# Strided attention pairs: two residues in one product of 36 columns

## The chip, the cores and the metric

The kernel runs on one core of a Trainium2 chip. The metric is the device time of one execution in microseconds (us). The engines are TensorE (PE, with PEld for its weight loads), VectorE (DVE), ScalarE (ACT), GpSimd (POOL) and SyncE (SP), which issues most of the DMAs.

## The reference

Attention with 8 batches, 8 heads, 576 positions and 64 features a head, followed by a gated feed-forward layer. Half of the heads see the last 32 positions, the other half those positions that have the same residue modulo 32.

```python
def _attn_ref(q, k, v):
    B, H, S, D = q.shape                       # 8, 8, 576, 64
    scores = (1.0 / np.sqrt(D)) * np.matmul(q, k.transpose(0, 1, 3, 2))
    pos = np.arange(S)
    rel = pos[:, None] - pos[None, :]
    mask_local = (rel >= 0) & (rel < 32)
    mask_strided = (rel >= 0) & (pos[None, :] % 32 == pos[:, None] % 32)
    masks = np.stack([mask_local if h < H // 2 else mask_strided for h in range(H)], axis=0)
    scores = np.where(masks[None], scores, -1000000000.0)
    scores = scores - np.max(scores, axis=-1, keepdims=True)
    attn = np.exp(scores)
    attn = attn / (np.sum(attn, axis=-1, keepdims=True) + 1e-09)
    return np.matmul(attn, v).astype(np.float32)

def _moe_ref(x, w_in, w_out):                  # x: 4608 x 512, w_in: 512 x 2048, w_out: 2048 x 512
    h = x @ w_in
    g = h * np.clip(h + 3.0, 0.0, 6.0) / 6.0
    return (g @ w_out).astype(np.float32)
```

## The kernel before, in words

**Attention** goes by pairs of heads: four pairs a batch, two local and two strided, 32 in all. `kept_pair(g)` records all the steps of one pair. A strided pair's sequence is sorted by residue: 32 residues with 18 positions each (`NPOS`), padded to 32 rows on the query side. Eight blocks of four residues make 128 rows. For one block, one residue and one head there is one score product, 32 queries by 18 keys (L676, in `scores`): 8 * 4 * 2 = 64 products. Head `j` takes rows 64j to 64j+63 of the array and writes bank `ps[j]`. Batches 0 and 1 are done in ways of their own (`early`, `apart`), which the change leaves. From batch 3 on (`ADDED`) the causal mask `mtri` is added on DVE while the scores leave their bank (`keep`, L687); in batch 2 a product with `eye` puts it into the bank first (L665), and a copy takes the scores out (L689 on ACT, L691 on DVE).

Then follow, on a tile `e` with 2 * 8 * 18 = 288 elements a partition: maximum (`most`, L730, DVE), subtraction (`less`, L752, POOL), exponential (L755, ACT), sum (`total`, L758, DVE), reciprocal (L762 and L763, DVE), scaling (`norm`, L767, POOL). Four 32-row transposes a head (L813, DVE) turn the result into the tile `at` for one head and `at2` for the other, four residues on the diagonal of a 128 by 128 block. The values are one product for each block and head, with 128 rows, 64 weight columns and 72 columns moved (L869, `both_mm`): 16 products into two banks, the first four blocks in one and the last four in the other. ACT and DVE write them out into `x`, or `xf` from batch 3 on (`keep_x`, L458, L469, L472). A local pair has twelve transposes (L808) and window products (L441) in their place. In batch 1 (`apart`), the strided values are 64 columns of weights over 18 rows with 18 columns moved (L881, `half_mm`), in two halves with a small DVE copy between them, the fence (L885).

**Feed-forward.** Batches 0 to 2 run alone (`ffn`): wide products of 128 by 512 in groups of three, L1030 to L1032 into the two banks `ph`, and L963 to L965 into the four banks `acc`. A gate on ACT and DVE (L1065, L1069) empties a `ph` bank into `u`; `split_g` makes a high part on ACT (L996) and a low part on POOL (L999). From 353 us on, batches go in pairs (`ffn_pair`, three pairs `0`, `1`, `2`), with seven combined products where there were eight (L1204 to L1206, two banks as well), whose sums DVE forms in `htmp` (L1223). `split_g` is told by the names `0a`, `0b`, `1a`, `1b` which half it serves; the last pair has a splitting routine of its own and doesn't call it.

**Order.** Every step is recorded by `op(engine, cost, function, reads, writes, due, ...)`; `Plan.emit` then simulates the engines with these costs and due times and fixes one order for each engine, ahead of time. Some steps may go to either of two engines, as the plan finds them free. On the chip each engine runs its order strictly, and waits for semaphores. Due times follow from `T0` (the start of the first feed-forward), `TILE` and the lists above. So a changed cost shifts many steps by some places on every engine.

Of the kernel before, what the change touches and what calls it, by code (L numbers as in the profile page):

```python
# [20 lines left out]
P = 128  # L21
# [4 lines left out]
NQB = 6  # L26
NPOS = 18
RB = 7
SB = RB * NPOS
# [15 lines left out]

T0 = 36.0
TILE = 98.5
# [31 lines left out]
PORT = ("DVE", "POOL")  # L79
IDLE_DVE = ("2a", "2b")  # L80

# [131 lines left out]
def attention_ffn(ctx: ExitStack, tc, q, k, v, w_in, w_out, out):  # L213
# [40 lines left out]
    mturn = const.tile([PAD, 2 * PAD], BF16, name="mturn")  # L254
    mtri = const.tile([P, NPOS], BF16, name="mtri")
    mwhole = const.tile([QB, NQB, 2 * PAD], BF16, name="mwhole")
    left = [const.tile([P, B * LEFT], F32, name=f"left{c}") for c in range(NCC)]
# [10 lines left out]
    def masks():  # L268
# [16 lines left out]
        for a in range(4):  # L285
# [3 lines left out]
                base=0, pattern=[[-1, NPOS]], channel_multiplier=1)  # L289

    op("POOL", 0.8, identity, writes=[("ident",)], due=-100)
    op("POOL", 2.2, masks, reads=[("ident",)], writes=["const"], due=-22)

# [185 lines left out]
    def kept_pair(g):  # L479
# [146 lines left out]
        n = QB if loc else P  # L626
        w = 2 * PAD if loc else NPOS
        cols = nblk * w

        def e_both():  # L630
            t = e_tile()
            return t[:QB, :, :cols].rearrange("p j (u x) -> p j u x", x=w) if loc else \
                t[:, :, base:base + 8 * PAD].rearrange("p j (u x) -> p j u x", x=PAD)[:, :, :, :w]
# [25 lines left out]
        def scores():  # L659
            if spare_e and loc:  # L660
                tiles["e", loc] = new(wp, ekey, [P, 2, cols], F32, f"e{nm}")
            ps = [psum(sb[j], f"ps{nm}{j}")[:n, :cols].rearrange("p (u x) -> p u x", x=w) for j in range(2)]
            m = (mband if loc else mtri).unsqueeze(1).to_broadcast([n, nblk, w])
            for j in range(0 if added else 2):
                nc.tensor.matmul(ps[j], eye[:n, :n], m, start=True, stop=False)  # L665
            if loc and not added:
                for j in range(2):
                    m = mturn if shifted else mfirst
                    nc.tensor.matmul(ps[j][:PAD, 0, :m.shape[1]], eye[:PAD, :PAD], m, start=False, stop=False)
            for i in range(nblk):  # L670
                for a in range(n // PAD):
                    for j in range(2):
                        own = slice(D * j, D * j + D)
                        r = i * (n // PAD) + a
                        k0 = max(r, 1 if shifted else 0) * (PAD if loc else NPOS)
                        nc.tensor.matmul(ps[j][PAD * a:PAD * a + PAD, i], qk_of("q")[own, PAD * r:PAD * r + PAD],  # L676
                                         qk_of("k")[own, k0:k0 + w], start=added, stop=added or i == nblk - 1)
# [4 lines left out]
        def keep(e, j):  # L682
            ps = ps_of(j)
            if j == 0:
                new(ap, stkey, [P, 2, 2, 8], F32, f"st{nm}")
            if added:
                nc.vector.tensor_tensor(out=e_own(j), in0=ps, in1=mwhole if loc else mtri.unsqueeze(1).to_broadcast([n, nblk, w]), op=ALU.add)  # L687
            elif e == "ACT":
                nc.scalar.copy(e_own(j), in_halves(ps))  # L689
            else:  # L690
                nc.vector.tensor_copy(e_own(j), in_halves(ps))  # L691
# [28 lines left out]
        if early and not loc:  # L720
            sb = []
        else:
          op("PE", ((1.35 if loc else 1.35) if early else (1.1 if loc else 1.35) if added else 1.5) * slow, scores, reads=["const", qkey, kkey, *both_halves], writes=[*sb, ekey, ekey1, stkey],
             take=sb, due=sd - 1000, room=0.0 if early else ROOM, mode="s", words=4 * 2 * (18 if loc else 32) + 6)
        for j in range(len(sb)):
# [72 lines left out]
        def transposes(j):  # L798
            def tr():
                e = e_whole(j)  # L800
                if apart:
                    nc.vector.transpose(tiles["atk"][:, odd, j], e)
                    return
                at = tiles[akeys[j]]
                if loc:
                    for a in range(3):
                        for h in range(2):
                            nc.vector.transpose(at[PAD * (a + h):PAD * (a + h) + PAD, :, PAD * a:PAD * a + PAD],  # L808
                                                e[PAD * a:PAD * a + PAD, :, PAD * h:PAD * h + PAD])
                else:  # L810
                    for a in range(4):
                        rows = slice(PAD * a, PAD * a + PAD)
                        nc.vector.transpose(at[rows, :, rows], e[rows])  # L813

            op("DVE", 6 * 0.37 if loc else 0.45 if apart else 4 * 0.435, tr, reads=[ekey, ekey1, *home], writes=[akeys[j]], due=due - 2 + j)
# [48 lines left out]
        else:  # L864
            def both_mm():
                ps, vt = [psum(vb[h], f"pv{nm}{h}") for h in range(2)], tiles[vkey]
                for i in range(8):
                    for j in range(2):
                        nc.tensor.matmul(ps[i // 4][D * j:D * j + D, i % 4 * P:i % 4 * P + 4 * NPOS], vt[:, j, i],  # L869
                                         (tiles[akeys[i % 2]][:, 4 * j + i // 2] if early else tiles[akeys[j]][:, i]).rearrange("p (a m) -> p a m", a=4)[:, :, :NPOS], start=True, stop=True)  # L870

            def half_mm(u):
                if u == 0:
# [14 lines left out]
            if apart:  # L888
                op("PE", 0.65 * slow, partial(half_mm, 0), reads=[*akeys, *home, vkey], writes=vb, take=vb,
                   due=due - 1002, room=0.0 if early else ROOM, mode="v", words=130)  # L890
                op("DVE", 0.16, fence, reads=vb, writes=[stkey], due=due - 1002)
                op("PE", 0.65 * slow, partial(half_mm, 1), reads=[*akeys, *home, vkey], writes=[*vb, *xk, lk], due=due - 1001, mode="v", words=130)
            else:
                op("PE", 1.3 * slow, both_mm, reads=[*akeys, vkey], writes=[*vb, *xk, lk], take=vb,
                   due=due - 1001, room=0.0 if early else ROOM, mode="v", words=64)
            puts = []
            for h in range(2):
                def what(ps, m):
                    if apart:
                        return ps[:, :16 * NPOS].rearrange("c (t a m) -> c t a m", t=RUN, a=2)[..., m]  # L900
                    return ps.rearrange("c (t x) -> c t x", x=P)[:, :, :4 * NPOS].rearrange("c t (a m) -> c t a m", a=4)[..., m]

                def place(x, h=h):
                    if apart:
                        return x.rearrange("c (m a z t) -> c t a z m", t=RUN, a=2, z=2)[:, :, :, h]
                    return x.rearrange("c (m a t) -> c t a m", t=RUN, a=4)[:, 4 * h:4 * h + 4]
# [640 lines left out]
    op("POOL", 0.1, first_tiles, writes=["plain"], due=-30)  # L1547
    zero(("e",), ap, [P, 2, 5 * P], F32, 1.45, -12, "e")
    op("POOL", 0.0, lambda: None, reads=[("e",)], writes=["el", "es", "el1", "es1"], due=-12)
# [36 lines left out]
    def homes():  # L1586
        tiles["sq"] = new(wp, homes_at[0], [P, 8 * P], F32, "sq")
        tiles["sv"] = new(wp, homes_at[1], [P, 2, 8, D], F32, "sv")
        tiles["at2"] = new(wp, homes_at[2], [P, 8, P], F32, "at2")
        tiles["at"] = new(ap, ("at",), [P, 8, P], F32, "at")  # L1590
    hk = ["sq", "sv", "at2", "at"]
# [61 lines left out]
```

## Time and profile before

| | |
|---|---|
| time, median of 3 runs | 885.27 us (883.56 to 891.9) |
| the profiled execution's own time | 883.06 us |
| its span, first to last instruction | 881.3 us |
| granted TensorE clock | 1.000 |
| PE / DVE / POOL / ACT busy | 98% / 71% / 52% / 46% of the span |
| matrix products | 8046 records |
| DMA | 190.73 MB, mean 216 GB/s |

The profile shows one execution. An engine's busy time is the sum of its instructions without overlap; a matrix product's row has an end that is modelled, so two products that follow each other overlap in it, and the pace is read from their starts. A row of the timeline gives start, duration, engine, line, operation, output and inputs, the part of the array (`64*32`: 64 rows, 32 weight columns), the moved tile and how many of them were merged. A row of the groups gives the same with busy time, mean ns of one, and idle time of the engine before them with its releasers. One fp32 product shows as two records there.

### The profile page before, as it was taken

To read this page: it belongs to the slowest core of one execution; us is meant where nothing else is said; L and a number is where in the kernel's file an instruction comes from. 1 tells how busy PE (TensorE), PEld (TensorE's weight loads), DVE (VectorE), ACT (ScalarE), POOL (GpSimd) and SP (SyncE) were. 2 spreads that over 40 slices of the span, in tenths; PEclk is the share of its full clock that TensorE was granted. 3 is DMA by queue.
4 is the path that set the end of the run, shared out by engine and by line. 5 is a ranking of instruction groups with operands and counts; after the bars stand their busy time and mean duration, and the time that the engine had idled before them with its cause. 6 is when DMAs were issued, how large, how long until landed. Compare 5 with 4: busy or idle time off the path is not lost.

```text
span 881.3 us, 20423 instructions
## 1 busy us (share of the span) xinstructions
PE 867.9 (98%) x8046; PEld 712.3 (81%) x8046; DVE 626.6 (71%) x1014; ACT 401.9 (46%) x723; POOL 458.4 (52%) x402
## 2 busy tenths in 40 slices
PE   9999999999999999999999999999999999999998
PEld 6777788788787888788888888888887888888898
DVE  6999977678888878766768733546658756566872
ACT  4787564333344434534345632544455343333730
POOL 5797666329777638222234844434559973131300
PEclk9999999999999999999999999999999999999999
DMA  7988836875789899887774688789738789565632
GB/s 186 318 234 210 194 99 182 253 199 166 209 236 237 239 231 224 255 232 205 215 218 142 200 283 219 252 236 254 246 130 316 264 286 328 168 214 192 188 126 70
DMA packets 231825, 190.73 MB, mean 216 GB/s; under 512 B 164401, under 2 KB 195121, under 8 KB 231729
## 3 DMA queue, kind: packets, MB, share of 16 engines
q1 hardware_dynamic: 231572, 189.12, 74.1%
q8 instruction: 64, 1.05, 0.5%
q10 hardware_dynamic: 156, 0.29, 0.1%
q14 instruction: 33, 0.26, 0.1%
HBM read 148.47 MB, written 40.89 MB: 215 GB/s over the span
## 4 chain that ended last, share of the span: by engine, by line
PE 87%; DVE 5%; DMA 3%; SPq 2%; POOL 2%; issue 1%; ACT 1%; DVEq 0%; ACTq 0%; POOLq 0%
PE ph L1204 9%; PE ph L1205 8%; PE ph L1206 8%; PE ph L1030 5%; PE acc L963 4%; PE ph L1032 4%; PE ph L1031 4%; PE acc L965 4%; PE acc L964 4%; PE az L1425 3%; PE az L1423 3%; PE az L1424 3%; PE ps L676 3%; DMA rawi<-in_moe_w_in_dram 2%; PE pv L441 2%; PE acc0a L963 2%
## 5 line engine op out<-in xcount | busy, mean ns | idle before, releaser
L1204 PE MATMUL ph<-xc,wi 128*128 128x512 f32 x336 | 134.4, 400 | 2.4 <-DVE u L1069 1.8
L1205 PE MATMUL ph<-xc,wi 128*128 128x512 f32 x336 | 131.4, 391 | 0.3 <-issue 0.3
L1206 PE MATMUL ph<-xc,wi 128*128 128x512 f32 x336 | 131.0, 390 | 0.0
L1223 DVE TENSOR_TENSOR htmp<-ph,htmp 128x512 f32<-128x512 f32 x72 | 49.5, 688 | 75.1 <-PE ph L1206 70.2
L999 POOL TENSOR_TENSOR g<-u,g 128x512 fp32r<-128x512 f32 x48 | 64.7, 1349 | 55.8 <-ACT g L996 27.4
L1030 PE MATMUL ph<-x,wi 128*128 128x512 f32 x192 | 78.5, 409 | 0.9 <-DVE u L1069 0.9
L1204 PEld LDWEIGHTS ph<-xc,wi 128*128 128x128 f32 x336 | 63.1, 188 | 19.2 <-DVE htmp L1217 2.8
L963 PE MATMUL acc<-wo,g 128*128 128x512 f32 x192 | 76.5, 398 | 0.5 <-ACT g L996 0.5
L965 PE MATMUL acc<-wo,g 128*128 128x512 f32 x192 | 75.0, 391 | 0.9 <-POOL g L999 0.9
L1031 PE MATMUL ph<-x,wi 128*128 128x512 f32 x192 | 75.0, 391 | 0.0
L1032 PE MATMUL ph<-x,wi 128*128 128x512 f32 x192 | 75.0, 390 | 0.0
L964 PE MATMUL acc<-wo,g 128*128 128x512 f32 x192 | 74.9, 390 | 0.0
L1206 PEld LDWEIGHTS ph<-xc,wi 128*128 128x128 f32 x336 | 63.1, 188 | 14.1 <-issue 0.5
L1205 PEld LDWEIGHTS ph<-xc,wi 128*128 128x128 f32 x336 | 63.3, 188 | 11.0
L808 DVE STREAM_TRANSPOSE atloc<-e 32x192 f32<-32x192 f32 x168 | 61.8, 368 | 7.9 <-POOL e L767 5.5
L1065 ACT ACTIVATE u<-ph,three 128x512 f32<-128x512 f32 x48 | 33.0, 687 | 73.7 <-PE ph L1032 73.5
L752 POOL TENSOR_TENSOR e<-e,st 128x288 f32<-128x288 f32 (+1 forms) x30 | 34.2, 1139 | 61.2 <-DVE st L730 61.1
L1215 ACT COPY htmp<-ph 128x512 f32<-128x512 f32 x56 | 32.8, 587 | 50.1 <-PE ph L1206 49.0
L813 DVE STREAM_TRANSPOSE at<-e 32x256 f32<-32x256 f32 x112 | 48.6, 434 | 5.2 <-POOL e L767 3.9
L996 ACT CAST g<-u 128x512 fp32r<-128x512 f32 x48 | 29.6, 620 | 38.0 <-DVE u L1069 28.9
L1030 PEld LDWEIGHTS ph<-x,wi 128*128 128x128 f32 x192 | 36.0, 187 | 10.7 <-DVE u L1069 2.3
L767 POOL TENSOR_TENSOR e<-e,st 128x288 f32<-128x288 f32 (+1 forms) x30 | 33.9, 1130 | 18.7 <-DVE st L763 15.3
(318 smaller groups left out, 2311.7 us busy)
## 6 DMA issues: line engine op xcount, KB each, us to landing
wi<-wid SPq DMA_DIRECT2D x84, 512.0 KB
wo<-wod SPq DMA_DIRECT2D x83, 512.0 KB
rawi<-in_moe_w_in_dram SPq DMA_DIRECT2D x16, 512.0 KB
rawo<-in_moe_w_out_dram SPq DMA_DIRECT2D x16, 512.0 KB
wod<-wo SPq DMA_DIRECT2D x16, 512.0 KB
wid<-st SPq DMA_DIRECT2D x64, 128.0 KB
qn<-in_q_dram SPq DMA_DIRECT2D x112, 72.0 KB
kn<-in_k_dram SPq DMA_DIRECT2D x112, 72.0 KB
```

The costliest lines, as they stand in the source:

```text
L808: nc.vector.transpose(at[PAD * (a + h):PAD * (a + h) + PAD, :, PAD * a:PAD * a + PAD], e[PAD * a:PAD * a + PAD, :, PAD * h:PAD * h + PAD])
L963: nc.tensor.matmul(acc, gh, woh, start=fc == 0, stop=False)
L964: nc.tensor.matmul(acc, gh, wol, start=False, stop=False)
L965: nc.tensor.matmul(acc, gl, woh, start=False, stop=end)
L999: on(e).tensor_tensor(out=to(1), in0=tiles[uk], in1=tiles[gk[0]].bitcast(F32), op=ALU.subtract)
L1030: nc.tensor.matmul(ph, wih, xh, start=n_ == 0, stop=False)
L1031: nc.tensor.matmul(ph, wih, xl, start=False, stop=False)
L1032: nc.tensor.matmul(ph, wil, xh, start=False, stop=n_ == NCC - 1)
L1204: nc.tensor.matmul(ph, w[:, j, 0], x[:, 0], start=u in (0, 1, 3) and j == 0, stop=False, skip_group_check=u in (2, 4, 5, 6))
L1205: nc.tensor.matmul(ph, w[:, j, 0], x[:, 1], start=False, stop=False, skip_group_check=u in (2, 4, 5, 6))
L1206: nc.tensor.matmul(ph, w[:, j, 1], x[:, 0], start=False, stop=j == 1, skip_group_check=u in (2, 4, 5, 6))
L1223: nc.vector.tensor_tensor(out=tiles[s.key], in0=tiles[bank], in1=tiles[s.key], op=ALU.add)
```

## The change

For the strided pairs of batches 2 to 7 (`wide`, 12 pairs) one score product takes two residues: 64 queries by 36 keys (`TWO`), 32 products in place of 64. Half of each result is masked, by the mask `mtwo`, built on POOL at the start. `e` then has 2 * 8 * 36 = 576 elements a partition. The transposes take each residue's own 18 columns (and 14 beside them) out of it. `at` and `at2` shrink to blocks of two residues, 64 rows high, and the values become 32 products with 64 rows, 64 weight columns and 36 columns moved (`two_mm`), with all first halves of the blocks in one bank and all second halves in the other.

The recorded costs of the two product steps go down, from 1.35 to 0.8 (batch 2: 1.5 to 1.05) and from 1.3 to 0.75, `T0` goes from 36 to 37, and `IDLE_DVE`, the names for which `split_g` may use DVE for the low part, from `2a`, `2b` (which never reach `split_g`) to `0b`, `1a`, `1b`. Every other cost that depends on the number of columns follows by its formula.

```diff
+TWO = 2 * NPOS
-T0 = 36.0
+T0 = 37.0
-IDLE_DVE = ("2a", "2b")
+IDLE_DVE = ("0b", "1a", "1b")
...
+        nc.gpsimd.memset(mtwo, NEG)
+        for a in range(4):
+            m = slice(PAD * a, PAD * a + PAD)
+            nc.gpsimd.tensor_copy(mtwo[m, a % 2 * NPOS:a % 2 * NPOS + NPOS], mtri[m])
...
-        w = 2 * PAD if loc else NPOS
+        wide = not loc and b > 1
+        w = 2 * PAD if loc else TWO if wide else NPOS
...
-            m = (mband if loc else mtri).unsqueeze(1).to_broadcast([n, nblk, w])
+            m = (mband if loc else mtwo if wide else mtri).unsqueeze(1).to_broadcast([n, nblk, w])
...
-            for i in range(nblk):
+            for i in range(nblk if wide else 0):
+                for a in range(2):
+                    for j in range(2):
+                        own, r = slice(D * j, D * j + D), 4 * i + 2 * a
+                        nc.tensor.matmul(ps[j][2 * PAD * a:2 * PAD * a + 2 * PAD, i], qk_of("q")[own, PAD * r:PAD * r + 2 * PAD],
+                                         qk_of("k")[own, NPOS * r:NPOS * r + TWO], start=added, stop=added or i == nblk - 1)
+            for i in range(0 if wide else nblk):
...
-          op("PE", ((1.35 if loc else 1.35) if early else (1.1 if loc else 1.35) if added else 1.5) * slow, scores, ...
+          op("PE", (0.8 if added else 1.05) if wide else (1.35 if early else 1.1 if added else 1.5) * slow, scores, ...
...
+                elif wide:
+                    for a in range(4):
+                        rows, at0 = slice(PAD * a, PAD * a + PAD), base + a % 2 * NPOS
+                        nc.vector.transpose(at[rows, :, PAD * (a % 2):PAD * (a % 2) + PAD],
+                                            e_tile()[rows, j, at0:at0 + nblk * TWO].rearrange("p (u x) -> p u x", x=TWO)[:, :, :PAD])
...
+            def two_mm():
+                vt = tiles[vkey]
+                for h in range(2):
+                    psum(vb[h], f"pv{nm}{h}")
+                for t in range(8):
+                    for j, half in ((0, 0), (1, 1), (0, 1), (1, 0)):
+                        rows = slice(D * half, D * half + D)
+                        nc.tensor.matmul(tiles[vb[half].key][D * j:D * j + D, TWO * t:TWO * t + TWO], vt[rows, j, t],
+                                         tiles[akeys[j]][rows, t].rearrange("p (z m) -> p z m", z=2)[:, :, :NPOS], start=True, stop=True)
...
+            elif wide:
+                op("PE", 0.75, two_mm, reads=[*akeys, vkey], writes=[*vb, *xk, lk], take=vb,
+                   due=due - 1001, room=ROOM, mode="v", words=128)
...
-        tiles["at2"] = new(wp, homes_at[2], [P, 8, P], F32, "at2")
-        tiles["at"] = new(ap, ("at",), [P, 8, P], F32, "at")
+        tiles["at2"] = new(wp, homes_at[2], [P, 8, 2 * PAD], F32, "at2")
+        tiles["at"] = new(ap, ("at",), [P, 8, 2 * PAD], F32, "at")
```

Two places of the order. First TensorE at the values of batch 3's first strided pair. `pv_20` and `pv_21` are the two banks, `at` and the other `at` tile the two heads, `sv` the values; the last row shown of each is one of more that repeat. Before, the 16 products come between two `acc` groups, first those of one bank:

```order
L965 MATMUL acc_0_2409<-wo_1715,g_11_3369 128x512
L869 MATMUL pv_20_3391<-at,sv 64x72
L869 MATMUL pv_20_3391<-at_2187,sv 64x72
...
L869 MATMUL pv_21_3392<-at,sv 64x72
L869 MATMUL pv_21_3392<-at_2187,sv 64x72
```

Now 32 products, four to a block, which take turns at banks and heads:

```order
L1070 MATMUL ph_14_3341<-x_00_1826,wi_1795 128x512
L900 MATMUL pv_20_3369<-at,sv 64x36
L900 MATMUL pv_21_3370<-at_2171,sv 64x36
L900 MATMUL pv_21_3370<-at,sv 64x36
L900 MATMUL pv_20_3369<-at_2171,sv 64x36
```

The block stands one feed-forward chunk later than before (ahead of the `acc` groups of chunk 12), and each bank is now written until the block's last products.

Second, DVE at the end of batch 2's feed-forward. `u_15` is the gate of its last chunk, `st_2` and `ps_20`, `ps_21` belong to a strided pair, the two rows `atloc` are six transposes each of a local pair, `htmp` the first sum of the first pair of batches. Before:

```order
L687 TENSOR_TENSOR e<-ps_20_4882,mtri 128x8x18
L687 TENSOR_TENSOR e<-ps_21_4883,mtri 128x8x18
L730 TENSOR_REDUCE st_2_4960<-e 128x16
L808 STREAM_TRANSPOSE atloc_879<-e 32x6x32 x6
L808 STREAM_TRANSPOSE atloc_772<-e 32x6x32 x6
L1069 SCALAR_TENSOR_TENSOR u_15_4989<-u_15_4989,ph_15_4833 128x512
L758 TENSOR_REDUCE st_2_4960<-e 128x16
```

Now:

```order
L1186 TENSOR_TENSOR hxf_3325<-hxf_3325 128x512
L1107 SCALAR_TENSOR_TENSOR u_15_4800<-u_15_4800,ph_15_4734 128x512
L1180 TENSOR_TENSOR xc_5_4812<-hxf_3325,xc_5_4812 128x512
L703 TENSOR_TENSOR e<-ps_20_4814,mtwo 128x288
L703 TENSOR_TENSOR e<-ps_21_4815,mtwo 128x288
L746 TENSOR_REDUCE st_2_4863<-e 128x16
L824 STREAM_TRANSPOSE atloc_885<-e 32x6x32 x6
L824 STREAM_TRANSPOSE atloc_778<-e 32x6x32 x6
L1261 TENSOR_TENSOR htmp_2958<-ph_0_1_4880,htmp_2958 128x512
```

The gate moved ahead of the twelve transposes, and the first sum `htmp` stands directly behind them.

More of the change, by code (lines that the diff above doesn't have):

```diff
@@ L255, in attention_ffn @@
     mtri = const.tile([P, NPOS], BF16, name="mtri")
+    mtwo = const.tile([P, TWO], BF16, name="mtwo")
     mwhole = const.tile([QB, NQB, 2 * PAD], BF16, name="mwhole")
@@ L289, in masks @@
                 base=0, pattern=[[-1, NPOS]], channel_multiplier=1)
+        nc.gpsimd.memset(mtwo, NEG)
+        for a in range(4):
+            m = slice(PAD * a, PAD * a + PAD)
+            nc.gpsimd.tensor_copy(mtwo[m, a % 2 * NPOS:a % 2 * NPOS + NPOS], mtri[m])
     op("POOL", 0.8, identity, writes=[("ident",)], due=-100)
-    op("POOL", 2.2, masks, reads=[("ident",)], writes=["const"], due=-22)
+    op("POOL", 2.8, masks, reads=[("ident",)], writes=["const"], due=-22)
     def whole_mask():
@@ L631, in e_both @@
             t = e_tile()
+            if wide:
+                return t[:, :, base:base + cols].rearrange("p j (u x) -> p j u x", x=w)
             return t[:QB, :, :cols].rearrange("p j (u x) -> p j u x", x=w) if loc else \
@@ L686, in keep @@
             if added:
-                nc.vector.tensor_tensor(out=e_own(j), in0=ps, in1=mwhole if loc else mtri.unsqueeze(1).to_broadcast([n, nblk, w]), op=ALU.add)
+                nc.vector.tensor_tensor(out=e_own(j), in0=ps, in1=mwhole if loc else (mtwo if wide else mtri).unsqueeze(1).to_broadcast([n, nblk, w]), op=ALU.add)
             elif e == "ACT":
@@ L722, in kept_pair @@
         else:
-          op("PE", ((1.35 if loc else 1.35) if early else (1.1 if loc else 1.35) if added else 1.5) * slow, scores, reads=["const", qkey, kkey, *both_halves], writes=[*sb, ekey, ekey1, stkey],
-             take=sb, due=sd - 1000, room=0.0 if early else ROOM, mode="s", words=4 * 2 * (18 if loc else 32) + 6)
+          op("PE", (0.8 if added else 1.05) if wide else (1.35 if early else 1.1 if added else 1.5) * slow, scores, reads=["const", qkey, kkey, *both_halves], writes=[*sb, ekey, ekey1, stkey],
+             take=sb, due=sd - 1000, room=0.0 if early else ROOM, mode="s", words=4 * 2 * (18 if loc else 16 if wide else 32) + 6)
         for j in range(len(sb)):
@@ L799, in tr @@
             def tr():
-                e = e_whole(j)
+                e = None if wide else e_whole(j)
                 if apart:
@@ L898, in what @@
                 def what(ps, m):
+                    if wide:
+                        return ps[:, :RUN * TWO].rearrange("c (t z m) -> c t z m", t=RUN, z=2)[..., m]
                     if apart:
@@ L903, in place @@
                 def place(x, h=h):
+                    if wide:
+                        return x.rearrange("c (m a z t) -> c t a z m", t=RUN, a=2, z=2)[:, :, h]
                     if apart:
@@ L1547, in attention_ffn @@
     op("POOL", 0.1, first_tiles, writes=["plain"], due=-30)
-    zero(("e",), ap, [P, 2, 5 * P], F32, 1.45, -12, "e")
+    zero(("e",), ap, [P, 2, 6 * 2 * PAD + NPOS + RUN * TWO + 2], F32, 1.55, -12, "e")
     op("POOL", 0.0, lambda: None, reads=[("e",)], writes=["el", "es", "el1", "es1"], due=-12)
```

## The prediction

> **What bounds the kernel now.** I read the page first (busy shares, then the chain that ended last), then TensorE's list of waits.
>
> ```profile
> PE 867.9 (98%) x8046; PEld 712.3 (81%) x8046; DVE 626.6 (71%) x1014; ACT 401.9 (46%) x723; POOL 458.4 (52%) x402
> PE 87%; DVE 5%; DMA 3%; SPq 2%; POOL 2%; issue 1%; ACT 1%; DVEq 0%; ACTq 0%; POOLq 0%
> PE ph L1204 <- DVE u L1069: 1.8, 1, 1.8
> PE pv L881 <- DVE st L885: 1.1, 1, 1.1
> ...
> PE kp L542 <- DMA kn<-in_k_dram: 0.7, 1, 0.7
> ...
> PE kp L542 <- issue: 0.2, 1, 0.2
> ```
>
> TensorE (PE) is busy 867.9 of 881.3 us, and it holds 87% of the chain. Its waits are twelve rows, of which the first, two in the middle and the last are shown; together they are 9.7 us. So two things can shorten this kernel: less TensorE work, and those few waits. Work added to VectorE (DVE), GpSimd (POOL) or ScalarE (ACT) costs nothing until TensorE has to wait for it. The only DMA that TensorE waits for is the first one.
>
> **The products.** What a block of small products costs is the time by which it pushes apart the wide products around it. Timeline of TensorE around a strided pair's scores, around a pair's values, and around one half of a second-batch pair's values (L881):
>
> ```profile
> 200.61 0.39 PE L965 MATMUL acc<-wo,g 128*128 128x512 f32 x1
> 200.93 1.27 PE L676 MATMUL ps<-kplain,sq 64*32 64x18 f32 x128
> ...
> 202.46 0.39 PE L1031 MATMUL ph<-x,wi 128*128 128x512 f32 x1
> 202.69 0.39 PE L1032 MATMUL ph<-x,wi 128*128 128x512 f32 x1
> ...
> 230.02 0.39 PE L965 MATMUL acc<-wo,g 128*128 128x512 f32 x1
> 230.34 1.22 PE L869 MATMUL pv<-at,sv 128*64 128x72 f32 x32
> ...
> 231.82 0.40 PE L964 MATMUL acc<-wo,g 128*128 128x512 f32 x1
> ...
> 70.09 0.39 PE L1032 MATMUL ph<-x,wi 128*128 128x512 f32 x1
> 70.41 1.12 PE L881 MATMUL pv<-atkept,v 18*64 18x18 f32 x64
> ...
> 71.81 0.40 PE L1031 MATMUL ph<-x,wi 128*128 128x512 f32 x1
> ```
>
> Wide products follow each other by 0.23 us (202.46 to 202.69), so two steps are 0.46. Scores: 202.46 - 200.61 - 0.46 = 1.39 us. Values: 231.82 - 230.02 - 0.46 = 1.34. The block of L881: 71.81 - 70.09 - 0.46 = 1.26.
>
> Now the count. A product shows as two records (the strided scores have 64 products and 128 records). 64*32 in a row is the part of the 128*128 array that holds the weights; eight such parts fit, and since 128 records start within 1.27 us, 9.9 ns apart, the parts work side by side. Of 128*64 there are two. Before, scores are 128 records over eight parts, or 16 rounds of 1.27/16 = 79 ns; values are 32 records over two parts, 16 rounds of 1.22/16 = 76 ns. After, both are 64 records of 64*64 over four parts: 16 rounds again. The number of products halves in one and doubles in the other, but **the number of rounds stays**, and the price of a round decides. L881 is the nearest row: 64 records, 64 weight columns, four parts in use, and the parts in the order that the new values have. Its round is 1.12/16 = 70 ns. It moves 18 columns where the new ones move 36; L869 moves 72 in a round of 76 ns, so 36 lies between 70 and 76. The weight loads say why wider weights aren't free (groups by shape; the mean ns of one stands after the busy time):
>
> ```profile
> L676 PEld LDWEIGHTS ps<-kplain,sq 64*32 64x32 f32 x1536 | 14.0, 105 | 3.8 <-issue 3.6
> L881 PEld LDWEIGHTS pv<-atkept,v 18*64 18x64 f32 x256 | 4.2, 133 | 2.6 <-DVE st L885 1.5 <-issue 0.7 <-ACT g L996 0.4
> L1204 PEld LDWEIGHTS ph<-xc,wi 128*128 128x128 f32 x336 | 63.1, 188 | 19.2 <-DVE htmp L1217 2.8 <-DVE u L1069 2.2 <-DVE htmp L1223 1.1
> ```
>
> 32, 64 and 128 weight columns take 105, 133 and 188 ns: some 0.86 ns a column beside a fixed part, whatever the rows. So half as many loads of twice the columns save the fixed part alone. I take 70 ns, so 1.26 us a block: scores save 0.13, values 0.08, a pair 0.21, the 12 strided pairs of batches 2 to 7 together 2.5 us. The bounds: with 76 ns a round a block costs 1.26 + 0.10 = 1.36, and a pair saves nothing (0.03 - 0.02); with the scores' present 1.27/128 = 9.9 ns a record, 64 records are 0.63, a block is 1.26 - 0.49 = 0.77, and a pair saves 0.62 + 0.57 = 1.19, in all 14.3.
>
> [...]
>
> Batch 2 puts its mask in by a product, whose columns double. Rows of the first batch (288 columns) and of batch 2 (144):
>
> ```profile
> 8.42 0.41 PE L695 MATMUL ps<-mtri,eye 128*128 128x288 bf16 x2
> 8.76 1.11 PE L699 MATMUL ps<-kplain,qt 64*128 64x72 f32 x16
> ...
> 145.40 0.30 PE L665 MATMUL ps<-mtri,eye 128*128 128x144 bf16 x2
> 145.63 1.27 PE L676 MATMUL ps<-kplain,sq 64*32 64x18 f32 x128
> ```
>
> 0.34 against 0.23 us: 0.11 more, twice: 0.2 us.
>
> **Elementwise work, off TensorE's path.** A block of two residues has 36 columns of which half are masked, so a partition's elements double, 144 to 288 a head. By shape, strided now and the local pairs' larger one:
>
> ```profile
> L687 DVE TENSOR_TENSOR e<-ps,mtri 128x144 f32<-128x144 f32 x20 | 5.4, 300 | 9.7 <-PE ps L676 9.6
> L687 DVE TENSOR_TENSOR e<-ps,mwhole 96x384 f32<-96x384 f32 x20 | 10.4, 547 | 7.3 <-PE ps L676 7.0
> L730 DVE TENSOR_REDUCE st<-e 128x16 f32<-128x288 f32 x16 | 7.2, 448 | 2.0 <-ACT e L689 1.7
> L730 DVE TENSOR_REDUCE st<-e 96x12 f32<-96x768 f32 x14 | 13.2, 940 | 3.7 <-ACT e L689 3.4
> L752 POOL TENSOR_TENSOR e<-e,st 128x288 f32<-128x288 f32 x16 | 12.1, 759 | 25.6 <-DVE st L730 25.5
> L752 POOL TENSOR_TENSOR e<-e,st 96x768 f32<-96x768 f32 x14 | 22.0, 1574 | 35.6 <-DVE st L730 35.5
> L755 ACT ACTIVATE e<-e 128x288 f32<-128x288 f32 x16 | 7.1, 446 | 5.9 <-POOL e L752 5.9
> L755 ACT ACTIVATE e<-e 96x768 f32<-96x768 f32 x14 | 11.8, 845 | 3.6 <-POOL e L752 3.6
> L1223 DVE TENSOR_TENSOR htmp<-ph,htmp 128x512 f32<-128x512 f32 x72 | 49.5, 688 | 75.1 <-PE ph L1206 70.2 <-ACT htmp L1215 4.6
> ```
>
> On straight lines between the two shapes, at the new size: a mask addition 448 ns (+0.15, two of them), a reduction 743 (+0.30, two), a POOL operation 1248 (+0.49, two), the exponential 685 (+0.24). A pair: DVE +0.89, POOL +0.98, ACT +0.24; twelve pairs: 10.7, 11.8 and 2.9 us. The chain from scores to values grows by 2.1 us; what hides it is the distance between them, 29.4 us (200.93 to 230.34). What hides DVE's share: L1223, the addition on which the pair stages' banks come free, finds DVE idle 75.1/72 = 1.04 us before each, and a piece of 0.15 or 0.30 fits in that. Without that cover each pair would cost its 0.89. Transposes and evacuations keep count and size: nothing.
>
> `IDLE_DVE` lets DVE do a subtraction that POOL did; the new order has 14 of them on DVE. POOL's row, and DVE's rows for such an operation alone and beside POOL's traffic:
>
> ```profile
> L999 POOL TENSOR_TENSOR g11b<-g,g01b 128x512 fp32r<-128x512 f32 x16 | 24.3, 1528 | 0.8 <-ACT g01b L996 0.8
> L1388 DVE TENSOR_TENSOR gz<-ua,gz 128x512 fp32r<-128x512 f32 x4 | 2.7, 683 | 0.0
> L1142 DVE TENSOR_TENSOR xc<-hxf,xc 128x512 fp32r<-128x512 f32 x15 | 20.2, 1356 | 2.3 <-ACT xc L1139 2.3
> 7.54 0.96 POOL L793 MEMSET at<- 128x1024 f32 x1 [1.08 <-PE kp L542]
> ```
>
> That is 14 times 0.68 to 1.36, 9.6 to 19.0 us more on DVE, and 21.4 less on POOL: DVE goes from 71 to 73 or 74%, POOL down by one. Both leave idle time, so nothing again. The new mask's five small operations at the start fall where POOL waits 1.08 us (last row), ahead of the first mask product at 8.42. Loads move by a few places on SP's queue; TensorE waits for none of the moved ones now, so I add nothing.
>
> **The waits.** The order moves two of them. DVE's and TensorE's timeline at the end of batch 2's feed-forward, and TensorE's at the second half of L881:
>
> ```profile
> 351.47 4.57 DVE L808 STREAM_TRANSPOSE atloc<-e 32x192 f32<-32x192 f32 x12 [0.73 <-POOL e L767]
> 356.07 0.69 DVE L1069 SCALAR_TENSOR_TENSOR u<-u,ph 128x512 f32<-128x512 f32 x1
> 356.81 0.50 PE L1204 MATMUL ph<-xc,wi 128*128 128x512 f32 x1 [1.78 <-DVE u L1069]
> 96.51 0.69 PE L881 MATMUL pv<-atkept,v 18*64 18x18 f32 x29 [1.07 <-DVE st L885]
> ```
>
> The gate `u_15` stands behind twelve transposes, and TensorE waits 1.8 us for the bank that it reads. After, it stands ahead of them. Next late on DVE is the addition that frees the other bank, `htmp<-ph_0_1`, which now follows the transposes. TensorE wants that bank 14 groups of three wide products (3 * 0.23 = 0.69 each) and one block of scores after the last product that `u_15` needs: 9.7 + 1.26 = 10.9 us. On DVE stand ahead of it the gate (0.69, and as much for its relu), `xc_5` (1.36), two mask additions (0.9), a reduction (0.74), the transposes (4.57) and itself (0.69): 9.6 us. It fits with 1.3 us to spare, so I count **-1.8**; a miss gives back up to 1.8. The other one, L881, waits for the fence L885: the reciprocal and a transpose now follow it, but a weight join and a gate stand before it. Between -1.1 and +1.1; nearest to its present row, 0.
>
> **Sum**, against the profiled execution's own 883.06 us (881.3 of span and 1.8 around it): -2.5 + 0.2 - 1.8 = -4.1, 879.0. The median of before, 885.27, stands 2.2 above its profiled execution, and the lowest run 0.5 above; I put the median of after at 880.
>
> **Rivals.** *Products, not rounds, are what costs.* For it: the scores' record takes 9.9 ns, less than any other here, so records can follow each other faster than L881's do. Against it: L881 itself has as many records as the new blocks and takes 17.5 ns for each. It gives 883.06 - 14.3 + 0.2 - 1.8 = 867.2. [...]
>
> *DVE comes late at the gates* (the slower side). Place: batches 3 to 7, where a local pair's twelve transposes (4.57 us) with the wider reductions or a moved subtraction behind them can stand ahead of the operation that frees a bank. Price: 1.8 us each time, as at 356. From three on it is slower than before (-4.1 + 5.4); with six, of some ten such blocks, 879.0 + 10.8 = 889.8. For it: DVE takes 20 to 30 us more. Against: this happened once in before, with DVE at 71%.
>
> *Nothing moves*: a round at 76 ns and a new wait where one goes: 883.3.
>
> **Chances.** The forecast (with the nothing-moves case, 875 to 885): 0.77; products cost: 0.12; DVE late: 0.11, half of it near 886 and half near 890 or over. The range 870 to 889 leaves out the first rival and the worst of the second. One per cent is about what a measurement of this kernel can tell from no change. Faster by more (under 876.4 against 885.27): 0.12 and 0.06 of the forecast's lower edge, 0.18. Slower by more (over 894.1): 0.04. Within: 0.78.
>
> **What would show it.** In the profile after: blocks of 64 records of some 1.1 to 1.2 us for scores and for values (0.6 if the first rival holds); mask additions near 448, reductions near 743, POOL near 1248 ns; no wait of L1204 for `u` at the change to pairs; DVE at 73 to 74%; TensorE's idle time below 12 us. The prediction is wrong if a round is far from 70 ns, or if TensorE's waits differ from before by more than some 4 us.

## The result and the profile after

The changed kernel takes 896.4 us, median of ten runs (892.73 to 900.15), against 887.62 for ten runs of the kernel before beside it (883.56 to 891.9): ratio 1.0091 [1.0065, 1.0117]. 880.0 and a range of 870 to 889 were predicted. The profiled execution took 896.36, 13.3 us more than before's, at a mean granted clock of 0.992.

The page's first part, and the first, second and fourth to sixth rows of TensorE's waits:

```profile
PE 874.0 (98%) x7662; PEld 714.0 (80%) x7662; DVE 625.0 (70%) x1006; ACT 403.8 (45%) x725; POOL 474.1 (53%) x413
PE ph L1068 <- DVE u L1107: 4.9, 4, 1.7
PE az L1463 <- DVE hs L1426: 1.8, 1, 1.8
...
PE acc0a L1003 <- POOL g10a L1037: 1.2, 1, 1.2
PE acc L1001 <- ACT g L1034: 1.1, 2, 0.7
PE acc0a L1001 <- ACT g00a L1034: 1.1, 1, 1.1
```

TensorE's idle time rises from 13.4 to 20.5 us (span less busy). At L1068, the first product of a `ph` group, it now waits 4.9 us for gates (`u`); before, it waited 0.9 us at the same line (L1030 there) and 1.8 us at L1204. A clock of 0.992 over 894.5 us is another 7 us, an estimate from these two numbers. The new products are as priced. TensorE's timeline at a block of scores:

```profile
205.52 0.39 PE L1003 MATMUL acc<-wo,g 128*128 128x512 f32 x1
205.84 1.14 PE L684 MATMUL ps<-kplain,sq 64*64 64x36 f32 x64
206.91 0.50 PE L1068 MATMUL ph<-x,wi 128*128 128x512 f32 x1
207.24 0.39 PE L1069 MATMUL ph<-x,wi 128*128 128x512 f32 x1
```

207.24 - 205.52 - 0.46 = 1.26 us. The elementwise groups after: DVE's mask addition and reduction, POOL's subtraction, and ACT's exponential of a local pair and of a strided one.

```profile
L703 DVE TENSOR_TENSOR e<-ps,mtwo 128x288 f32<-128x288 f32 x20 | 8.3, 451 | 16.7 <-PE ps L684 16.7
L746 DVE TENSOR_REDUCE st<-e 128x16 f32<-128x576 f32 x12 | 9.0, 749 | 0.2
L768 POOL TENSOR_TENSOR e<-e,st 128x576 f32<-128x576 f32 x12 | 14.9, 1241 | 20.0 <-DVE st L746 19.8
L771 ACT ACTIVATE e<-e 96x768 f32<-96x768 f32 x14 | 11.8, 845 | 15.3 <-POOL e L768 6.3 <-DVE at L829 6.0 <-POOL e L783 3.0
L771 ACT ACTIVATE e<-e 128x576 f32<-128x576 f32 x12 | 8.2, 682 | 11.6 <-POOL e L768 7.4 <-DVE e L703 4.1
```

The durations are the predicted ones. Strange is what ended the idle time of the fourth row. A local pair's exponential reads and writes its own part of `e`, which POOL's subtraction made ready; before, that was its only releaser (3.6 us, POOL L752). Now it is released by L829, the transposes of a *strided* pair, which read another part of `e`, and by L783, the scaling of a strided pair. The timeline of DVE, ACT and POOL around the largest of these waits, with the product of TensorE behind it:

```profile
266.19 1.17 POOL L783 TENSOR_TENSOR e<-e,st 128x576 f32<-128x576 f32 x1
267.43 1.47 POOL L768 TENSOR_TENSOR e<-e,st 96x768 f32<-96x768 f32 x1
268.94 3.60 DVE L829 STREAM_TRANSPOSE at<-e 32x256 f32<-32x256 f32 x8 [3.30 <-POOL e L768]
270.37 0.85 ACT L771 ACTIVATE e<-e 96x768 f32<-96x768 f32 x1 [5.99 <-DVE at L829]
271.12 0.67 ACT L1103 ACTIVATE u<-ph,three 128x512 f32<-128x512 f32 x1
272.58 0.69 DVE L1107 SCALAR_TENSOR_TENSOR u<-u,ph 128x512 f32<-128x512 f32 x1
273.32 0.50 PE L1068 MATMUL ph<-x,wi 128*128 128x512 f32 x1 [1.20 <-DVE u L1107]
```

The transposes need the scaling L783, done at 267.36, but start at 268.94, when the local subtraction L768 is done. The local exponential needs L768, done at 268.90, but starts at 270.37, among the transposes. The gate `u` stands behind the transposes on DVE and starts at 272.58; TensorE waited 1.2 us for it.

These waits come from one line of the diff that the prediction left out: tile `e` goes from 640 to 692 elements a head (`[P, 2, 6 * 2 * PAD + NPOS + RUN * TWO + 2]`). A local pair uses elements 0 to 383 of each head, a strided one 384 to 689; nothing overlaps. Yet in the built program's instruction list, which names the semaphores that each instruction waits for, 11 of POOL's operations on `e` wait for DVE and POOL together (2 before), and 5 exponentials wait for DVE (1 before). With 704 elements a head it is 1 and 0, and every engine's order stays the same. At the exponential above, the lists of the two widths differ by the wait for DVE (`DVE_49` and `Pool_49` are a semaphore of DVE's and one of POOL's):

```
692:  L771 ACTIVATE e<-e 96x2x384 [waits DVE_49,Pool_49]
704:  L771 ACTIVATE e<-e 96x2x384 [waits Pool_49]
```

Waits between parts that don't overlap are called false waits below.

### The profile page after: what moved, and what is told of

Its sections match the earlier page's. It is cut to its first block, busy times and chain, and to the rows that moved or that the text cites. A ratio compares the mean times of both kernels' runs of the same rounds, so it can differ in the third digit from the quotient of the medians.

```text
span 894.5 us, 19674 instructions
## 1 busy us (share of the span) xinstructions
PE 874.0 (98%) x7662; PEld 714.0 (80%) x7662; DVE 625.0 (70%) x1006; ACT 403.8 (45%) x725; POOL 474.1 (53%) x413
## 4 chain that ended last, share of the span: by engine, by line
PE 86%; DVE 5%; POOL 2%; DMA 2%; issue 2%; SPq 1%; ACT 1%; DVEq 0%; POOLq 0%; ACTq 0%
PE ph L1242 9%; PE ph L1243 8%; PE ph L1244 8%; PE acc L1001 4%; PE ph L1068 4%; PE acc L1003 4%; PE acc L1002 4%; PE ph L1070 4%; PE ph L1069 4%; PE az L1463 3%; PE az L1461 3%; PE az L1462 3%; PE pv L448 2%; PE acc0b L1001 2%; PE acc0b L1002 2%; PE acc0b L1003 2%
## 5 line engine op out<-in xcount | busy, mean ns | idle before, releaser
L1068 PE MATMUL ph<-x,wi 128*128 128x512 f32 x192 | 78.3, 408 | 5.0 <-DVE u L1107 4.9
L768 POOL TENSOR_TENSOR e<-e,st 96x768 f32<-96x768 f32 (+2 forms) x30 | 41.2, 1373 | 46.3 <-DVE st L746 43.7
L783 POOL TENSOR_TENSOR e<-e,st 96x768 f32<-96x768 f32 (+2 forms) x30 | 38.9, 1296 | 30.5 <-DVE st L779 18.4
L1068 PEld LDWEIGHTS ph<-x,wi 128*128 128x128 f32 x192 | 36.2, 188 | 15.5 <-DVE u L1107 7.6
L829 DVE STREAM_TRANSPOSE at<-e 32x256 f32<-32x256 f32 x96 | 41.7, 434 | 9.5 <-POOL e L783 5.0
L1037 POOL TENSOR_TENSOR g10a<-u,g00a 128x512 fp32r<-128x512 f32 x16 | 21.1, 1317 | 47.2 <-ACT g00a L1034 38.5
```

What stands on the lines that cost most here:

```text
L1037: on(e).tensor_tensor(out=to(1), in0=tiles[uk], in1=tiles[gk[0]].bitcast(F32), op=ALU.subtract)
L1068: nc.tensor.matmul(ph, wih, xh, start=n_ == 0, stop=False)
```

## The experiments

The first four asked whether the order or the arithmetic makes the loss. First, the changed arithmetic with a plan that is told all of before's numbers, so that the engines run in before's order:

```diff
-T0 = 37.0
+T0 = 36.0
-IDLE_DVE = ("0b", "1a", "1b")
+IDLE_DVE = ("2a", "2b")
-op("PE", (0.8 if added else 1.05) if wide else
+op("PE", (1.35 if added else 1.5) if wide else
-op("PE", 0.75, two_mm
+op("PE", 1.3, two_mm
-pool = 0.12 + 0.00355 * cols
+pool = 0.12 + 0.00355 * told
...
```

(`told` is the 144 columns of before; the lines for the mask addition, the reductions and the exponential change in the same way.)

> The changed arithmetic (two residues in one product, 288 elements a head, two_mm) in the order of the kernel before: the plan is given the numbers that it had before (product steps 1.35, 1.5 and 1.3, elementwise costs for 144 columns, T0 36, the old IDLE_DVE), so every engine has its steps in the order of before. Theory 'order' (the new order makes TensorE wait, and the waits lower its clock): the time falls to that of before less what TensorE saves, 0.995 to 1.0 of before, TensorE's waits 10 to 13 us, clock 1.000 in a quiet execution. Rival 'work' (the wider elementwise steps come late whatever the order): 1.005 to 1.012, with TensorE waiting for DVE's gates some 8 us more than before.

907.48 us, 1.0245 [1.0194, 1.0296]: slower than either theory allowed. Second, the reverse: before's arithmetic, and a plan that is told the changed numbers (the lines above the other way, in the kernel before).

> The arithmetic of the kernel before in the order of the changed kernel: the plan is given the changed kernel's numbers (product steps 0.8, 1.05 and 0.75, elementwise costs for 288 columns, T0 37, the new IDLE_DVE). Theory 'order': as slow as the changed kernel or a little slower, since its products take 2.4 us more, 1.008 to 1.014 of before, with waits at the same places (272, 285 and 310 us) and a clock of 0.989 to 0.998. Rival 'work': as before, 0.998 to 1.004, since the narrow steps have their old lengths.

889.79, 1.0034 [0.9994, 1.0073]. So it is the arithmetic (with the tile that comes with it) that loses, and the changed kernel's own order wins back more than half of it. Third, the changed kernel with measured product costs:

```diff
-op("PE", (0.8 if added else 1.05) if wide else
+op("PE", (1.27 if added else 1.4) if wide else
-op("PE", 0.75, two_mm
+op("PE", 1.27, two_mm
```

> The changed kernel with the two product steps told to the plan as they measured: 1.27 (batch 2: 1.4) for scores in place of 0.8 (1.05), 1.27 for values in place of 0.75; T0 and IDLE_DVE as changed. Theory 'wrong costs' (the plan runs ahead of TensorE by half a microsecond a step, so elementwise steps stand too early on DVE's queue): the waits at 272 to 357 us go, 0.995 to 1.002 of before. Rivals 'work' and 'other settings' (T0, IDLE_DVE): no change against the changed kernel, 1.006 to 1.012.

887.66, 1.0005 [0.9983, 1.0027]. Fourth, the changed kernel with the two old settings:

```diff
-T0 = 37.0
+T0 = 36.0
-IDLE_DVE = ("0b", "1a", "1b")
+IDLE_DVE = ("2a", "2b")
```

> The changed kernel with T0 and IDLE_DVE as before, the new product costs kept. Theory 'other settings': the waits go, 0.995 to 1.002 of before. Rivals 'wrong costs' and 'work': 1.005 to 1.012 as the changed kernel, waits for gates still there.

895.23, 1.0106 [1.006, 1.0151]. So the two settings aren't the cause, while the two product costs, which change nothing except the order, take the loss away. That suggested theory 1: a longer elementwise chain keeps DVE standing, gates come late, and more so where the costs are understated (1a).

**Pieces.** The longer elementwise work alone, in the kernel before and in its order (`e_wide` has 36 columns a block, and `e` 672 elements):

```diff
-nc.vector.tensor_reduce(out=st_of(0), in_=e_both(), axis=AX.X, op=ALU.max)
+nc.vector.tensor_reduce(out=st_of(0), in_=e_wide(), axis=AX.X, op=ALU.max)
-            x = e_both()
+            x = e_wide()
...
```

(The subtraction, the exponential, the sum and the scaling likewise.)

> The kernel before, with its products, its plan's numbers and its order, but in the strided pairs of batches 2 to 7 the maximum, the subtraction, the exponential, the sum and the scaling work on 36 columns a block in place of 18 (their values are then not those of the reference; the mask additions keep 18). DVE gets +0.6 us a pair, POOL +0.98, ACT +0.24, and the plan isn't told. Theory 1 (the longer elementwise chain, unknown to the order, makes DVE come late at the gates; it is what the wide kernel in before's order lost 2.45% by): slower by 1.5 to 2.5%, 900 to 909 us, waits of ph for u of several us. Theory 2 (the loss comes from the new products: each bank of the values is held until the block's end, scores in blocks of two residues): within 0.4% of before, 884 to 890. Prediction's own step (elementwise costs nothing): the same as theory 2.

894.37, 1.0075 [1.0046, 1.0104]: theory 1 holds in kind, with half of its size or less. Rows of TensorE's waits:

```profile
PE ph L1035 <- DVE u L1074: 3.8, 5, 1.1
PE ph L1209 <- DVE u L1074: 1.8, 1, 1.8
...
PE ph L1209 <- DVE htmp L1228: 1.5, 3, 0.8
```

Before had 0.9 us of the first (prediction's page: L1030) and nothing of the third. Next, the new values alone in the kernel before (scores and lengths as before, `at` in blocks of two residues):

```diff
-op("PE", 1.3 * slow, both_mm, ...
+op("PE", 1.3 * slow, two_mm if b > 1 else both_mm, ...
```

> The kernel before, with its plan's numbers and order, and only the values of the strided pairs of batches 2 to 7 in 32 products of 64 by 64 by 36; scores and elementwise work as before. Theory 1: the products are worth 0.08 us a pair, 1 us in all, and nothing else changes: 0.1% faster, 885 to 887 against 887. Theory 2 (both banks of the values held to the end of the block make the evacuation late): slower by 0.5 to 1.5%, new waits for banks behind L469 to L472.

890.57, 1.0047 [1.0021, 1.0074]. Neither theory saw this; TensorE's timeline shows a wait without a releaser, behind a block of the *old* scores:

```profile
320.43 1.27 PE L676 MATMUL ps<-kplain,sq 64*32 64x18 f32 x128
326.02 0.59 PE L1044 MATMUL ph<-x,wi 128*128 128x512 f32 x1 [4.33 <-issue]
```

This program holds the old 64 score products and the new 32 of values. What stalls it stays open; the changed kernel has no such row over 0.2 us. Then, in the changed kernel, costs halfway:

```diff
-op("PE", (0.8 if added else 1.05) if wide else
+op("PE", (1.0 if added else 1.2) if wide else
-op("PE", 0.75, two_mm
+op("PE", 1.0, two_mm
```

> The changed kernel with product costs halfway between its own and the measured ones (scores 1.0, batch 2 1.2, values 1.0 us; its own 0.8, 1.05, 0.75, measured 1.27, 1.4, 1.27). Theory 1a (the order is worse the more the plan understates the products): half of the loss, ratio 1.003 to 1.007, 890 to 893. Rival (any change of the numbers draws a new order, and orders differ by chance by up to 1%): anything from 0.998 to 1.012, without relation to the distance from the measured cost.

888.34, 1.0015 [0.9985, 1.0045]: less than the half that 1a expected, though the interval reaches it. Measured costs together with the old settings (both diffs from above):

> The changed kernel with the products' measured costs, and T0 and the subtraction's list as before. With the changed kernel (1.0091), its version with the old T0 and list (1.0106) and its version with measured costs (1.0005) this closes the square. Theory 1a (the costs decide, the two settings do nothing): within 0.4% of before, 884 to 890. Rival (measured costs need the new T0 and the moved subtractions as well): slower by 1% or more, 896 or over.

885.6, 0.9977 [0.9952, 1.0001]: the measured costs don't need the new settings. Now the wide kernel in before's order with the elementwise work on 18 of 36 columns:

```diff
-nc.scalar.activation(e_both(), e_both(), AF.Exp, scale=SCALE)
+nc.scalar.activation(e_half(), e_half(), AF.Exp, scale=SCALE)
...
```

(`e_half` is `e_both` on its first `NPOS` columns a block; the other five steps likewise.)

> The changed kernel's products in the order of before (as in the run that lost 2.45%), but mask addition, maximum, subtraction, exponential, sum and scaling of the wide strided pairs work on the first 18 of the 36 columns alone, so that they have the lengths of before (the values are then not those of the reference). Theory 1 (the longer elementwise chain makes that run's loss): back to 0.998 to 1.003, 882 to 887, waits of ph for u about 1 to 3 us. Theory 2 (the products in blocks make what the elementwise run didn't, 2.45 - 0.75): 1.012 to 1.02.

892.1, 1.0053 [1.0033, 1.0072]: the lengths are 1.9 of the 2.45 points, but 0.5 remain where before's waits should have come back. The same shortening in the changed kernel:

> The changed kernel itself, its order and plan's numbers, with the elementwise work of the wide pairs on the first 18 of the 36 columns alone (the values are then not those of the reference). Theory 1a (in this order the understated product costs make the loss: the mask additions stand too early in DVE's queue, DVE waits at them 33.0 us in all against 17.0 before): still slower by 0.5 to 0.9%, 891 to 894, DVE's idle time before the mask additions still 28 us or more. Rival (the elementwise lengths make it in this order too): within 0.3% of before.

889.42, 1.0021 [0.9997, 1.0044]: 1a predicted 0.5 to 0.9% and fell. The measured cost for the scores alone, and for the values alone:

> The changed kernel with the measured cost told for the strided scores alone (1.27, batch 2 1.4); the values keep 0.75. Theory 1a (mask additions queued too early because the scores are told too short): most of the loss goes, ratio 0.999 to 1.004, DVE's idle time before the strided mask additions 10 us or less in place of 16.7. Rival (it is the sum of what is understated that counts, or chance): 1.004 to 1.007, idle time between.

> The changed kernel with the measured cost told for the strided values alone (1.27); the scores keep 0.8 and 1.05. Theory 1a: most of the loss stays, ratio 1.006 to 1.01, DVE's idle time before the mask additions near 33 us. Rival (sum, or chance): 1.003 to 1.006 or anything else.

887.12, 1.0011 [0.9982, 1.0041], and 886.47, 0.9997 [0.9984, 1.0011]. Either half is enough, where 1a wanted the first to heal and the second not to. So the understated costs were no cause by themselves; another order merely hid one. The leftover of 0.5% sent me to the waits in the groups above, and to the width.

**The width.** First, before with one number changed:

```diff
-zero(("e",), ap, [P, 2, 5 * P], F32, 1.45, -12, "e")
+zero(("e",), ap, [P, 2, 5 * P + 52], F32, 1.45, -12, "e")
```

> The kernel before with one number changed: tile e is 692 elements a head wide in place of 640 (the 52 are never used). All operations, lengths and orders as before; the only change is that operations on one kind of pair's part of e get semaphore waits on operations of the other kind's part. Theory F (these false waits are a cause of the loss): ratio 1.004 to 1.010, 891 to 896, new waits of ph for u at 175, 226, 271 us. Rival E (only the lengths cost): within 0.2% of before.

896.04, 1.0089 [1.0059, 1.0119], for 52 elements that nothing uses. Its exponential of local pairs and two rows of TensorE's waits:

```profile
L755 ACT ACTIVATE e<-e 96x768 f32<-96x768 f32 x14 | 11.8, 846 | 7.2 <-DVE at L813 3.6 <-POOL e L752 2.4 <-DVE atkept L802 1.2
PE ph L1030 <- DVE u L1069: 4.0, 4, 1.4
PE ph L1204 <- DVE u L1069: 2.6, 1, 2.6
```

The foreign releaser is there, and 4.0 and 2.6 us of waits for gates where before had 0.9 and 1.8. The operations on `e` take no longer than at 640: the exponential 846 ns (845 before), a strided transpose 434 (434), POOL's subtraction of a local pair 1567 (1574). So it isn't that `e` is read or written more slowly at this width. Second, the changed kernel without that width:

```diff
-zero(("e",), ap, [P, 2, 6 * 2 * PAD + NPOS + RUN * TWO + 2], F32, 1.55, -12, "e")
+zero(("e",), ap, [P, 2, 704], F32, 1.55, -12, "e")
```

> The changed kernel with tile e 704 elements a head wide in place of 692; order, costs and lengths as in the changed kernel, the false waits gone. Theory F: most of the 0.91% goes, ratio 0.997 to 1.004, no wait of ph for u near 272 and 312 us. Rival E (the lengths, in this order): 1.006 to 1.010, these waits stay.

886.35, 0.9998 [0.9966, 1.0031]: the 0.91% is gone. Its profiled execution was the slowest of its ten (clock 0.990), but the place is clear. The same instructions as at 266 us above, then the group of the local pairs' exponential and those of the mask additions:

```profile
270.67 1.17 POOL L783 TENSOR_TENSOR e<-e,st 128x576 f32<-128x576 f32 x1
271.78 1.48 POOL L768 TENSOR_TENSOR e<-e,st 96x768 f32<-96x768 f32 x1
271.87 3.58 DVE L829 STREAM_TRANSPOSE at<-e 32x256 f32<-32x256 f32 x8 [1.74 <-POOL e L783]
273.30 0.85 ACT L771 ACTIVATE e<-e 96x768 f32<-96x768 f32 x1 [4.43 <-POOL e L768]
275.48 0.69 DVE L1107 SCALAR_TENSOR_TENSOR u<-u,ph 128x512 f32<-128x512 f32 x1
...
L771 ACT ACTIVATE e<-e 96x768 f32<-96x768 f32 x14 | 11.8, 845 | 10.3 <-POOL e L768 10.3
L703 DVE TENSOR_TENSOR e<-ps,mwhole 96x384 f32<-96x384 f32 x20 | 10.3, 547 | 16.3 <-PE ps L692 16.1
L703 DVE TENSOR_TENSOR e<-ps,mtwo 128x288 f32<-128x288 f32 x20 | 8.3, 452 | 16.7 <-PE ps L684 16.7
```

The transposes now start 0.03 us after their own scaling, the gate follows 3.6 us after that scaling where it took 5.2, and TensorE doesn't wait there. The exponential's only releaser is POOL's subtraction again. The last two rows close 1a: DVE stands at the mask additions the same 33.0 us that were its evidence, and the loss is gone. The wide kernel in before's order, 704 wide:

> The wide kernel in before's order (1.0245) with tile e 704 wide: false waits gone, lengths as in the changed kernel, the plan told before's numbers. Theory F with the lengths beside it: 1.006 to 1.013 (0.75% of the lengths, something for the longer mask additions, less 0.3% of the products). Rival (the two multiply: with the false waits gone the lengths are hidden): 0.998 to 1.004. Rival E (lengths alone): 1.02 or more.

896.36, 1.0102 [1.0052, 1.0152]. And the new products alone in that order (704, elementwise work on 18 columns):

> The new products in before's order and with before's numbers in the plan, tile e 704 wide (no false waits), elementwise work of the wide pairs on the first 18 of the 36 columns alone (the values are then not those of the reference): what the products save where nothing else changes. By the prediction's sum, -2.5 and +0.2: ratio 0.997, 882 to 885 against 887. Rival (products in blocks cost something of their own, as the run with the values alone, 1.0047, has it): 1.002 or over.

884.47 against 887.68, 0.9963 [0.9937, 0.999]. In before's order this makes a square:

| | e 704 wide | e 692 wide |
|---|---|---|
| elementwise on 18 columns | 0.9963 | 1.0053 |
| elementwise on 36 columns | 1.0102 | 1.0245 |

The width costs 0.9 and 1.4 points, the lengths 1.4 and 1.9, the products save 0.4. The four ratios have intervals of 0.2 to 0.5 points to either side, so whether width and lengths add or multiply stays open.

**The faster version.** Measured costs, old settings, 704 wide:

> The changed kernel with the products' measured costs told, T0 and the subtraction's list as before, and tile e 704 wide. Without the last its ratio was 0.9977 [0.9952, 1.0001]. Theory F: the products' 2.3 us come through, 0.994 to 0.998, 879 to 883 in a run at full clock. If the false waits were hidden in this order already: 0.997 to 1.000.

882.24 against 886.93, 0.9952 [0.9924, 0.998]; the lowest run is 879.2, before's 882.74. TensorE's page row and its longest waits:

```profile
PE 868.0 (99%) x7662; PEld 712.4 (81%) x7662; DVE 621.1 (71%) x1007; ACT 403.5 (46%) x723; POOL 476.9 (54%) x414
PE acc L1003 <- POOL g L1037: 1.5, 2, 0.9
PE ph L1242 <- DVE left L1186: 1.1, 1, 1.1
...
PE ph L1068 <- DVE u L1107: 0.9, 1, 0.9
```

It idles 10.7 us of its 878.7 and waits 0.9 for gates. The same with the changed kernel's `T0` and `IDLE_DVE`:

> As the version of 0.9952, but with T0 37 and the subtractions that the change lets DVE take. If the two settings do nothing: 0.994 to 0.997. If they cost (14 subtractions on DVE): 0.998 to 1.001.

883.07, 0.9965 [0.9939, 0.999]: the two settings can't be told apart from nothing. Both versions beat before; whether the measured costs add to 704 alone (0.9998) isn't settled, since the intervals overlap. Nor is it how much the width cost in these two orders: 0.9977 became 0.9952 and 1.0005 became 0.9965, with intervals that overlap too.

## Why the prediction was wrong

- *The products, -2.5 us: right.* A block costs 1.26 us as forecast, and the products alone give 0.9963, 3.3 us less [0.9 to 5.6]. The rival in which products and not rounds cost (867) is out.
- *Lengths: right* (451, 749, 1241 and 682 ns against 448, 743, 1248 and 685).
- *"Transposes and evacuations keep count and size: nothing", and of the waits only the two that "the order moves": the step that failed.* The transposes kept count and size and got new waits, as POOL's and ACT's operations on `e` did, from a width that the sum didn't contain. It is worth 0.9 points by itself (1.0089), and taking it out of the changed kernel takes 0.9 points away (1.0091 to 0.9998).
- *The elementwise work, counted at nothing: wrong too, as a rule.* The cover was read from TensorE (29.4 us between scores and values), but the chain passes DVE's queue, where gates stand behind transposes. In before's order the lengths cost 0.75% without the mask additions and 1.4 with them. The changed order, which knows the lengths, hides most of it: 0.9998 with 704, where the sum wanted 0.9954 (879.0 of 883.06).
- *The wait at 356, -1.8: went, but turned into another.* `u_15` holds nobody up any more; TensorE waits for `g` in its place, and the net is some -0.5:

```profile
356.71 0.50 PE L1001 MATMUL acc<-wo,g 128*128 128x512 f32 x1 [0.67 <-ACT g L1034]
...
358.06 0.49 PE L1003 MATMUL acc<-wo,g 128*128 128x512 f32 x1 [0.62 <-POOL g L1037]
```

- *L881: about right.* Its wait for the fence is gone, the lower end of the -1.1 to +1.1 given; the sum had it at 0.
- *14 subtractions on DVE: nothing, and no run speaks against it (0.9965 with them, 0.9952 without, `T0` changed along); DVE at 73 to 74%: wrong.* DVE is 70% busy, since the plan moved other work of its choice to POOL, for example `xc`, on DVE 15 times before and 11 after:

```profile
L1180 DVE TENSOR_TENSOR xc<-hxf,xc 128x512 fp32r<-128x512 f32 x11 | 13.6, 1245 | 1.2 <-ACT xc L1177 0.8
```

- *"TensorE's waits differ from before by more than some 4 us"* was given as what would prove it wrong: idle time rose by 7.1.
- *The rival "DVE comes late at the gates"* had the right mechanism: transposes ahead of a gate, three times between 268 and 313 us, 1.1 to 1.7 us each. (One of the three, 1.1 us at 286, has no part in the width: with 704 it is there too.) The rival was held at 0.11 because before showed it once. Before shows it with the width that makes no false waits, so that count said nothing of the change.

The two profiled executions don't divide the 13.3 us cleanly: some 7 are the clock, 7 the waits, less 2.3 of products. They also make the clock's part too large, since before's was taken at a clock of 1.000. The mean clock of 27 executions of before (those beside the 692 run) is 0.997, that of the changed kernel's ten 0.993. Span times clock, an estimate of the span at full clock, is 884 us in the mean for before, 888 for the changed kernel, 890 for before with 692, and 883 for the changed kernel with 704. So by this estimate the width costs 5 to 6 us at full clock, and the clock adds some 2 us to that. Why the clock was lower is only in part shown (see below).

## What to carry over

When a change moves lengths and strides of a shared tile, compare the semaphore waits of the two programs, not only their order: a part that overlaps nothing can still be waited for. Here four widths were run. With 640, 672 and 704 elements (before, the longer elementwise work alone, the changed kernel with 704) the idle time ahead of a local pair's exponential has POOL's subtraction as its only releaser (3.6, 4.9 and 10.3 us); with 692, DVE's transposes end 4.8 of 7.2 us of it in the kernel before and 6.0 of 15.3 us in the changed one. Which other widths have such waits isn't shown, nor why 692 has. In the groups, a releaser that neither writes what the operation reads nor uses what it writes is the sign. And work called hidden must be followed through the queue of the engine that does it, to what stands behind it there.

## What the runs showed of the hardware

TensorE's clock dropped after waits of 1.1 and 1.2 us. Four stretches of the changed kernel's profile, of 3.41 us each (busy time and count of PE, PEld, DVE, ACT and POOL, then granted clock, DMA share, GB/s):

```profile
496.08:499.49 3.41, 3.35 (x15) 2.44 (x13) 3.38 (x5) 1.56 (x3) 3.25 (x4) 1.00 0.14 36
499.49:502.90 3.41, 1.15 (x4) 0.67 (x5) 3.35 (x6) 1.48 (x3) 3.41 (x3) 1.00 0.88 263
502.90:506.31 3.41, 3.41 (x10) 2.63 (x9) 1.87 (x5) 1.79 (x3) 2.00 (x2) 0.50 0.76 290
506.31:509.72 3.41, 3.41 (x75) 2.69 (x74) 0.00 (x0) 0.57 (x2) 0.00 (x0) 1.00 0.80 256
```

Two waits of 1.1 and 1.2 us leave TensorE 1.15 us busy in the second stretch. The third runs at half clock (0.50): its wide products start 0.43 us apart (503.15 to 503.58) where 0.23 stood before, eight of them in the place of fifteen, by estimate some 1.6 us more (seven times 0.23). So here the waits cost more than their own length.

The two other half-rate places of this profile are 72.83 to 79.66, behind a wait of 0.85 us that ends at 70.21, and 745.25 to 748.66, behind one of 1.8 us that ends at 744.67. Other waits of such lengths have none behind them: in before's profile TensorE waits 0.86 us at the first of these places (until 69.52), in the changed kernel's 1.2 us until 273.32 and 1.7 us until 312.53, and the clock stays at 1.00 behind all three. What decides isn't shown. The ten executions of the changed kernel differ mainly by clock: their spans go from 890.9 to 898.4 us, span times clock only from 886.8 to 889.2.

This doesn't tie the clock to the width. None of the three places stands behind a wait that the width made; around those, from 265 to 320 us, the clock was 1.00. The profiled execution of before with 692 has a mean clock of 0.996, and where it was lower isn't shown.
